# A gated recurrence and a long convolution on one core: the hand-kept order table searched anew, with no state copy on VectorE

## The chip, the cores and the metric

The kernel runs on one core of one Trainium2 chip. The core has five engines that run at the same time, each through a queue of its own in order: TensorE (PE in the profile, its weight loads apart as PEld), VectorE (DVE), ScalarE (ACT), GpSimd (POOL) and SyncE (SP), which here only issues DMA transfers. TensorE writes to PSUM, eight banks of 2 KB a partition; GpSimd works in SBUF alone. The metric is the device time of one execution in microseconds, lower being better, as the median of several runs.

## The reference

Four sequences of 6272 steps with 256 channels. A gated recurrence runs over time; its state is the input of three projections; the middle one is convolved over the whole sequence (circularly, through an FFT) with a filter per channel; the three are multiplied, and an output projection follows.

```python
sig = 1.0 / (1.0 + np.exp(-f_logit))
f = lower_bound + (1.0 - lower_bound) * sig
for t in range(S):
    h = f[:, t] * h + (1.0 - f[:, t]) * x[:, t]
    y[:, t] = h
proj = y @ w_proj                      # [.., 768]: x1, x2, x3
X2 = np.fft.rfft(x2, n=S, axis=1)
H = np.fft.rfft(filter_fft, n=S, axis=0)
x2_conv = np.fft.irfft(X2 * H, n=S, axis=1)
out = (x1 * x2_conv * x3) @ w_out
```

## The kernel before

The work is cut into 2430 small operations, each made of one or a few instructions, and created stage by stage in `prepare`, `hgrn`, `gate`, `spectrum` and `phase_o` through `plan.op`. An operation knows which engines can do it (`cost` has a planner's figure for each) and which operations it needs before it. The string `ORDER` is the whole plan: three characters an entry give an operation's number, its engine and its PSUM bank. `emit` walks through the table and issues each operation on the engine named there, so the table alone sets what stands behind what in every queue. "MUL" as an engine means VectorE with the next product folded in: the entry that GpSimd would have done then issues nothing.

The stages for each of the four batches:

- `hgrn`: 13 chunks of 512 steps. Two loads (`load`, L357) bring gate logits and x; ScalarE takes the sigmoid (L360), GpSimd multiplies (L362, "u"), TensorE turns both so that time runs along the free dimension (L374), ScalarE or VectorE forms the gate (L387, L389), and VectorE scans (L395, in two halves of the channels). The state of the first 3072 steps is needed once more behind the end of the sequence; the operation "wrap" copies it there, from SBUF to SBUF, 512 f16 values a partition (the helper `copy`: L289 on ScalarE, L294 on VectorE, L301 on GpSimd).
- `spectrum`: the projection of the middle third (L729, `phase_p`), which needs all scans and wraps of the batch and the zero fills of the buffer X2 (`pads`, L335 to L339); then the first step of the transform over the 128 blocks (L742), the second (L804), the product with the filter's spectrum, either on VectorE straight out of PSUM (L827) or as an evacuation with a product on GpSimd (L836), and back (L846). The spectra of the filter wait in DRAM and are loaded a unit at a time (L782).
- `gate`: the projections x1 and x3 (L423), their evacuations (L291, L294, L296, `XS`) and their product `zt`, on VectorE from PSUM (L444) or on GpSimd (L453).
- `phase_o`: the last inverse step (L909), in 13 groups of rows, the multiply with `zt` on VectorE (L915), the output projection (L927), its evacuation and the store (L939).

While batch b is in `spectrum`, `gate` and `phase_o`, the loads, multiplies and scans of batch b+1 run between them. Ahead of all that, `prepare` makes the tables (sines, masks), scales the weights W13 and W2 (operation "W", L291, L296, L303) and takes the filter's spectrum: 13 loads (L640), a copy of each in SBUF ("fr", L289, L294, L301), a rotation on TensorE (L651), an evacuation into `f2` ("f2"), whose gaps a copy fills ("pad" in the table, from `iden`), and two transform steps (L666, L684). Meanwhile TensorE runs matmuls that compute nothing (L618).

The helper that many of the operations share (its scaled form is L291, L296 and L303):

```python
def copy(e, dst, src, scale=None):
    if e == "ACT":
        nc.scalar.copy(dst, src)
    elif e == "DVE":
        nc.vector.tensor_copy(dst, src)
    else:
        nc.gpsimd.tensor_copy(dst, src)
```

Of the kernel before, what the change touches and what calls it, by code (L numbers as in the profile page):

```python
# [24 lines left out]
M = 128  # L25
# [37 lines left out]
class Plan:  # L63
# [63 lines left out]
    "AAYA4gBAgAiQAPYACIA0gADIAQIBIgA8gAdQBEgAkQBQgBMgAbQA5YAcQA6QA1IDogBYgBUgAeSBBYAgSBggAhSARAATYBCSAzAABIAfUBcgA2UApWA7"  # L127
    "IBDCAWYAXYA9IA+WAjQBkgAmQA3MBFIDrgDpgBJYBKQDsgBGSBLAAsUAoUEDgDqgAtUD3gAxUBNYA/OBRIBSUAlQArQAUIBHKAEgBTEASABOQAZSBVYA"
    "aCD4gBPAAnTAvTAYIBZIBaUBbMAqTAVYBhYAyTBWSBXCEbgBdIAuQBiQEEgBjIBeUAwSBlYBfEEPgDtABmSBnKBvUBqSBwEBoQEQgDuYBrKBxUBpIB6S"
    "EngEcgByMEFABtQB0UBsYBuAAFYBzYB7KDvWB1MD5AB4SB/QB5CDzUCAAB8YDwODxOD6YCBSEzgAGgD0ECKQCCCD1MB9WEdACESB+GCLICDYEGYD7UCF"  # L130
    "KCIQD8ECRWD/SCJAD9MERACPQCMYE9gEogEAKCSGESYCNUCQAEHWELQE0gFHgEBKCOECaSEMAFIgEeYEIOEJOCbCEpAE+gENICUUCYSETWCZCCVECdSE"
    "KYCTYEXQCeCAJYEUOEVOChUEYACiME1ACfSEfWEZICcYAIYEWYCoUCgCEgOE/ACqQCpMEqYCjYEjSCrAEhOCkUFbgFSgEkCFRgCxQCvWClECHgElKFJA"
    "CwGE2YAKYCsYCGgB3gErUCyICtSEsMEtMEvQCuCC6WEwAC0SEiYC7GE3UExIC1CC4WE4ME6QC5GFdAE5MC9WFAYFlgFcgCzYC8YAMYDISC+GE7IE8IDB"
    "UFmgC3gAHgDJCFBWC/SFCOFDOFKYFEQDCEFTAC2gALYDACCWgDKUFFACngFvgDESDLEFGIFLWDDYDFCDNUDMYFUYFwgB2gDHgDPQDOEFOSFMOFNODQAJ"
    "SUFnAFeYFVQFPKFQKDRWJUEFWAFYUDSGFXIDaSFZEFoYFfWDbCFaMJTQFgGFiSJVAFhODUUF5gCmgCXgMWgDGgFjCAOYFpQDVEANYDTYFkKDhWFxAFqA"
    "D2YEuYJXUDiOFsSJZEFrIDYWFtCEmYFyYMigDfUF+gDZGFuKFzQDgEDdWEOYF0AF2UMjgEyAECAGkgMXgMugF1IDkSEaYDyYDcYD+YF3MJYQDlCJcRF4"
    "MGQUGRMDeGJWYJaAF6YJbYF7YDmgGMSGUWJeJGNKDngG2gMvgMYAGVGGSUGCQGYSGDAGZCGTMGOWGKUDWgMkAGPOMlYDjYMZYGEQGIWGWSGLEGGUGJOG"
    "XKGFAMwAGHMGAWJdQJhRGBGJfAJiSG/gGtgDXgJjJJkqGcWGdGGgUJgYGhEGaQGbIJmSGeWMxYJnTGfGF8UJoKGlQJpLF9EJrSGuWGpoJqYGiUJtCGyG"
    "JsTGjMJwRJxXGnoJuDHIUGmYJyBGoYGzYGqYGvYHJEG3SGwuHSgHbgGrQG5CGsAJzvGxYHAUG4YJvYG7qG0WHOQG1GJ0YG6YHBYG8YHCsJ1TJ2SHPAHK"
    "WJ3LJ6UHLGHEsHMQJ7THNAG9WJ8MHkgHtgJ9rJ4CHTUHQQJ/SKATHDYJ5YHFYG+GHXEHRIHVsHGQKBCHcWHHAHWYKCrHlUHguHeuHnEJ+YKESKFTKGCH"  # L140
    "UYHdYKJUHYYHhYIAgKHDH2QHZSHfYKIYH3AKLMHiWIJgHaCHpsHqYHoYHmYHuQHyoKDYHwoHjGKKUH8SKMEH4WH6UHzYH9CHvYKNYHxYKORH7EHrSISg"
    "H5OIbgKQBIBUHsCH+WIFsMaQIDEIKSMbAIEYH/OMeUIOCMcIH0WM6gMfEKPTH1GMgMIkQICYIPYILYITWIlAIGYM7gIugKRrIcUIXGIMqIHQKSYIeEKT"
    "XIIAINYIYYIUYJlYIgMKVHIVuMmSMqQMnCIQUNGgMrAIWYMoKNHgIZWIREI3gJAgMsIIaGIvUM8AKUSIoWIzsIfYIhYI0YIdYIpGKYTImQKWqKZVInAI"
    "qWIxsKXYKdSMVgNTgKaDIyYM9YIiQNSgIrOKfCKeTIjAKgrKbtMyWIsQNIAI4SMzGItIKhYM2UNJYI6CKiQKjRM0OM3EKnSNegJJgM4MM+WORgNfgKkA"
    "I8CIwYKpCKoQKlpKqoKrYI7YKcYI9YKmYI5YM/GNCUNogNpgKsRNDENAOI1SKuBKtQKxRI2CNEMNUAJBWNKSKvoKzBI+UNVYJFuNLCNOQJDGNMKJGYI/"
# [867 lines left out]
```

## Time and profile before

| | |
|---|---|
| median of 3 runs | 461.9 us (461.58 to 461.95) |
| profiled execution, its own time | 461.1 us |
| its span, first to last instruction | 459.3 us |
| mean granted TensorE clock | 0.994 |
| DMA | 119.05 MB, mean 259 GB/s |

The profiled execution is one run among others, 0.8 us below the median; its span leaves out 1.8 us around the first and the last instruction. Busy time is counted per engine; a busy TensorE is not TensorE at its peak, since matmuls overlap. In the slices of the whole span (40 of them, in tenths) TensorE is below nine tenths in three:

```profile
PE   7999999999999999999999999999799999999994
DVE  6889997999999995999999979999899958999873
POOL 6569996977998952678997826999696804868400
```

The first slice is the preparation, the last the end of the last batch, and the slice between them with a 7 lies at 321 to 333 us.

### The profile page before, as it was taken

Reading aid. Unit: us, or ns where it says so; the run is one execution under the profiler, and the core shown is the slowest. Engines: PE = TensorE matmul, PEld = TensorE weight load, DVE = VectorE, ACT = ScalarE, POOL = GpSimd, SP = SyncE. Lnnn points to the kernel's source line nnn. Section 1 sums busy time; section 2 is a strip of 40 time slices with the busy share of each in tenths; the row PEclk is TensorE's granted clock in tenths of the full one; section 3 lists DMA queues with packets and bytes.
Section 4 is the critical chain, followed back from the end, with each engine's and each line's share of the span. In section 5 each row is a group of like instructions: output and inputs, shape, how many; then the busy total and the mean of one; then the engine's idle time right before and its main releaser. Section 6 shows DMA issues by size and latency. Waiting matters only on the chain.

```text
span 459.3 us, 14550 instructions
## 1 busy us (share of the span) xinstructions
PE 439.4 (96%) x6013; PEld 346.3 (75%) x6013; DVE 411.8 (90%) x458; ACT 389.0 (85%) x539; POOL 326.0 (71%) x308
## 2 busy tenths in 40 slices
PE   7999999999999999999999999999799999999994
PEld 5877778777667889867668898786568897766783
DVE  6889997999999995999999979999899958999873
ACT  4589999989999879999999878999589878997553
POOL 6569996977998952678997826999696804868400
PEclk9999999999999999999999999999899999999999
DMA  8998899658998655588998381899837532752167
GB/s 323 407 395 330 288 392 386 266 184 272 349 335 285 259 199 214 195 295 297 298 330 309 151 324 46 271 360 380 321 81 261 202 138 100 241 179 94 48 269 293
DMA packets 42563, 119.05 MB, mean 259 GB/s; under 512 B 4096, under 2 KB 5760, under 8 KB 42496
## 3 DMA queue, kind: packets, MB, share of 16 engines
q1 hardware_dynamic: 42496, 118.11, 70.3%
q8 instruction: 47, 0.77, 0.7%
q14 instruction: 20, 0.16, 0.1%
HBM read 86.12 MB, written 31.98 MB: 257 GB/s over the span
## 4 chain that ended last, share of the span: by engine, by line
PE 66%; DVE 19%; issue 6%; ACT 6%; POOL 2%; DMA 1%; DVEq 0%; ACTq 0%; POOLq 0%
PE PS L423 15%; PE PS L846 9%; PE PS L729 8%; DVE HA L395 8%; PE PS L374 7%; PE PS L804 6%; PE PS L927 6%; PE PS L742 6%; DVE ys L915 5%; DVE zt L444 3%; PE PS L909 3%; PE PS L666 2%; ACT X L289 1%; PE PS L618 1%; PE PS L651 1%
## 5 line engine op out<-in xcount | busy, mean ns | idle before, releaser
L395 DVE TENSOR_TENSOR_SCAN HA<-fTs,HA,PS 128x512 f16<-128x512 f32 (+1 forms) x96 | 112.8, 1201 | 2.4 <-ACT fTs L387 1.5
L423 PE MATMUL PS<-HA,W 128*128 128x490 f16 (+1 forms) x416 | 102.9, 367 | 0.6 <-DVE XS L296 0.2
L836 POOL TENSOR_TENSOR PP<-HA,Hu 98x1008 f16<-98x1008 f16 x46 | 96.3, 2104 | 8.7 <-issue 7.0
L289 ACT CAST HA<-PS 98x512 f16<-98x512 f32 (+1 forms) x107 | 84.7, 819 | 5.6 <-PE PS L804 1.5
L362 POOL TENSOR_TENSOR XT<-XT,FL 128x1024 f32<-128x1024 f32 (+1 forms) x31 | 67.1, 2166 | 25.4 <-ACT FL L360 16.4
L387 ACT ACTIVATE fTs<-PS,nomc 128x512 f32<-128x512 f32 (+1 forms) x87 | 57.2, 666 | 10.0 <-PE PS L374 6.1
L915 DVE TENSOR_TENSOR ys<-PS,zt 128x1024 fp32r<-128x1024 f32 (+1 forms) x52 | 58.4, 1151 | 6.5 <-PE PS L909 2.9
L827 DVE TENSOR_TENSOR PP<-PS,Hu 98x1008 f16<-98x1008 f32 x50 | 59.0, 1198 | 1.5 <-PE PS L804 0.5
L927 PE MATMUL PS<-Wo,ys 128*128 128x256 f32 x392 | 57.7, 293 | 2.4 <-DVE ys L915 2.1
L846 PEld LDWEIGHTS <-PP 98*128 98x128 f16 x1024 | 50.2, 98 | 10.9 <-issue 2.6
L362 POOL TENSOR_TENSOR X<-X 128x1024 f32<-128x1024 f32 x21 | 49.9, 2383 | 10.8 <-ACT X L360 10.7
L846 PE MATMUL PS<-FT,PP 98*128 98x98 f16 x1024 | 56.2, 207 | 0.5 <-POOL PP L809 0.2
L423 PEld LDWEIGHTS <-W 128*128 128x128 f16 x416 | 34.5, 97 | 27.9 <-issue 4.4
L289 ACT CAST Th<-PS 128x784 f16<-128x784 f32 x61 | 49.6, 819 | 6.9 <-PE PS L846 5.6
L927 PEld LDWEIGHTS PS<-Wo,ys 128*128 128x128 f32 x392 | 49.5, 188 | 7.7 <-DVE ys L915 3.1
L444 DVE TENSOR_TENSOR zt<-PS,XS 128x490 f16<-128x490 f32 (+1 forms) x81 | 51.1, 648 | 4.4 <-PE PS L423 1.6
L291 ACT ACTIVATE XS<-PS 128x490 f32<-128x490 f32 (+1 forms) x79 | 45.3, 583 | 4.1 <-PE PS L423 3.1
L453 POOL TENSOR_TENSOR zt<-XS 128x490 f16<-128x490 f32 (+1 forms) x23 | 25.9, 1128 | 29.7 <-DVE ys L915 23.5
L729 PE MATMUL PS<-W,HA 128*128 128x256 f16 x392 | 43.8, 273 | 0.0
L729 PEld LDWEIGHTS <-HA 128*128 128x128 f16 x392 | 42.9, 142 | 0.6
L742 PEld LDWEIGHTS <-X 128*128 128x128 f16 x512 | 31.5, 98 | 9.3 <-issue 2.8
L294 DVE CAST X<-PS 128x1024 f16<-128x1024 f32 (+1 forms) x21 | 25.2, 1224 | 14.7 <-PE PS L729 13.3
(111 smaller groups left out, 801.4 us busy)
## 6 DMA issues: line engine op xcount, KB each, us to landing
Hu<-H SPq DMA_DIRECT2D x39, 512.0 KB, 5.4
FL<-in_f_logit_dram SPq DMA_DIRECT2D x27, 512.0 KB, 5.7
XT<-in_x_dram SPq DMA_DIRECT2D x27, 512.0 KB, 7.1
out_dram<-osb SPq DMA_DIRECT2D x24, 512.0 KB, 5.2
X<-in_f_logit_dram SPq DMA_DIRECT2D x21, 512.0 KB, 6.8
X<-in_x_dram SPq DMA_DIRECT2D x21, 512.0 KB, 6.9
out_dram<-PP SPq DMA_DIRECT2D x16, 512.0 KB, 5.2
Hl<-H SPq DMA_DIRECT2D x13, 512.0 KB, 4.3
```

What stands on the lines that cost most here:

```text
L289: nc.scalar.copy(dst, src)
L362: op("u", {"POOL": 0.1 + 0.553 * nb}, lambda e, xt=xt, ft=ft: nc.gpsimd.tensor_tensor(xt, xt, ft, op=AOP.mult), r=[("ft", k)], w=[("xt", k)])
L395: nc.vector.tensor_tensor_scan(h, fT, bank(pb)[:, 512 - hn:512 + hn], init, op0=AOP.mult, op1=AOP.add),
L423: nc.tensor.matmul(PS[:, p, 0:n], W13[:, kh, js], HA[:, HB[kh] + t0:HB[kh] + t0 + n], start=(kh == 0), stop=(kh == 1))
L444: nc.vector.tensor_tensor(zd(), px, xs(0), op=AOP.mult)
L729: nc.tensor.matmul(pp[:, r - r0, :], column(HB[kh], q_of(r)), W2[:, kh, :], start=(kh == 0), stop=(kh == 1))
L742: nc.tensor.matmul(pa[:, i, :], X2[:, j:j + 128], D1, start=True, stop=True)
L827: nc.vector.tensor_tensor(pr, px.unsqueeze(1).broadcast_to([TB, 2, UE, 63]), hh(), op=AOP.mult)
L836: nc.gpsimd.tensor_tensor(pr, spec[:, o, :, 1:64].unsqueeze(1).broadcast_to([TB, 2, UE, 63]), hh(), op=AOP.mult)
L846: nc.tensor.matmul(PS[:, ib + o, pr * TB:(pr + 1) * TB], PP[:TB, k, o, n, 2 * pr:2 * pr + 2, :], v[:TB], start=(n == 0), stop=(n == 1))
L915: nc.vector.tensor_tensor(late["ys"][:, yk, :, 0:rn * 128], PS[:, cb:cb + 2, 0:rn * 128], late["zt"][:].rearrange("p k r m -> p k (r m)") ...
L927: nc.tensor.matmul(po[:, i, :], late["ys"][:, yk, kh, i * 128:(i + 1) * 128], Wo[:, kh, :], start=(kh == 0), stop=(kh == 1))
```

## The change

The string `ORDER` is another one; nothing else in the file differs. The search that made the new table held every copy of VectorE from SBUF to SBUF while GpSimd works, and allowed no wrap on VectorE. The operations, their instructions and the buffers are the same; what differs is the engine of 156 of the 2430 operations, the order in the queues (of a TensorE operation by one place in the mean, at most 14), and the PSUM banks.

```diff
@@ -124,69 +124,69 @@
 ORDER = (
-    "AAYA4gBAgAiQAPYACIA0gADIAQIBIgA8gAdQBEgAkQBQgBMgAbQA5YAcQA6QA1IDogBYgBUgAeSBBYAgSBggAhSARAATYBCSAzAABIAfUBcgA2UApWA7"
...
+    "AAYAPYA4gA0gA5YABIACIADIAQIBAgBIgA8gA1ABMgBEgDogAiQAdQAkQAbQAcQAeQAgQA6QAhSAfSA2SARAATIA7IAWYAXABBYBCUBDEASAApWBJIAj"
...
 )
```

Read as operations, the changes of engine that are not paired off by a change back within the same kind are:

```text
wrap   batch 0: 2 from ACT to POOL     batch 3: 1 from DVE to POOL
W      DVE +1 (128x512, half of W13), POOL -1
pad    the filling of f2's gaps, ACT to DVE
masks  POOL to DVE (six instructions of one column)
fr     ACT +2, DVE -1, POOL -1
f2     ACT +2, DVE -2
A, Th  ACT +3, DVE -3
f      ACT +3, DVE -3
o      DVE +1, ACT -1
prod   ACT -2, DVE +1, MUL +1
xs     ACT -3, DVE -1, MUL +4
x2     batch 0: ACT +2, DVE -2; batches 2 and 3: DVE +1 and ACT -1 each
rest, idw, tabs   one each between ACT, DVE and POOL
```

On GpSimd the wrap of batch 3 that VectorE did stands behind the last multiply of that batch, ahead of the zero fills. In the last `phase_o`, TensorE's operations of row groups 9 to 11 stand so, before and after ("I1" is L909, "proj" L927, the number the row group):

```text
before  I1 9, proj 10, proj 9, I1 11, I1 12, proj 11, proj 12
after   I1 9, proj 10, I1 11, proj 9, proj 11, I1 12, proj 12
```

More of the change, by code (lines that the diff above doesn't have):

```diff
@@ L131 @@
[L131 to L145, printed above, removed]
@@ new lines @@
+    "WAmWAsWBKWA9YA+QAoUBFYA3KAVIAtUBQgBYgDpgBUgBggAZUBLGAzIA/IAxVAlVBGWBRABSQArVBcgBkgDrgDqgDsgEDgD3gAEgD4gEbgEEgEPgEcgA"
+    "nVBHGAaMBNIAvVAYYBOUBTABZIBaQAqWAyWAUYBhYBVIBWWAuSBiSBPEBXGBjCBdIBbIBeWBlYBmSAwQBfGDtABnKBqWBxSByKBoQBrOBpABvUBwMEFA"
+    "DuYBsYBzYAFYB6SBtWBuGB0UD5AB7KB1MDvQB4SDwIDxIB5CCBWDzUCCGEzgEQgD0EB/SCACD1MB8YD6YCKWEGYCDYB9QCLOCESD7UCFKEdAB+AD8ECI"
+    "WCJGD/QCPSERACQCCRWCSGD9MCNUEHSCOEEAIEBICUWCYQELUEIKEJKCVGCaWEeYCMYCTYCZAE1ACbGESYE0gEngCcYE2YCfQChSAHgE9gEogE+gFHgE"
+    "MMENMCiKCgAETWCdQEXUEpAEUOEVOAOYCjYEqYCeACoSEYECkQEZMCpCEfWClACvSEgOE/ACqUCrEEjQEkACwKEhOCxSErUCyKElICtWFJAEvSEsEEtM"
@@ new lines @@
+    "CuGC4QEwCExKE3WC6UAGgFIgFRgCsYFAYCzYC5AE4GC7EEiYEKYAIYC0QE5OE6SC1AC/UE7KDBWFTADAMDCGE8KFBQC9UFCAFEWC+EFKYFDIDKSC8YEW"
+    "YAJYAKYDDYFFGDIUDLCDJEDEQDFAALIFGOFSgB3gAMYEuYCXgFcgFUYB2gFbgCGgFlgFvgFmgC3gCWgFwgC2gFLSFOUFMKFNKFPEDPWDQGFdAFQMANYD"
+    "MYFeYDaQDNWFVSFYUFWKFXKDOGDbAFZEFnAFaMDRWJSQFfSJUADSGFxAJTRJXQJVBFiWFgKFjGDUUDVEJZIFhKFkOEOYFoYD2YDTYFyYFpQDhSFsUDfW"
+    "FqAFrIDiCDYSFtEDgGDZCFuMFzQDkWF0AF2SDdUCmgGkgMWgMXgCHgMigDXgMugDGgDlGDeEF5gDngMvgMYADWgCngDmgF+gMjgDHgF1IG2gGtgG/gEa"
+    "YDyYD+YEmYDcYDjYEyYECYJWYMZYF6YF7YJYQJcRF3KF4KGWSGSUGXCJeBJaoGUWGGSGQQGRIGVGGHCGTEGEWGISGMQGYUMwAGJCMkAGNAGFOGZMGKWG"
@@ new lines @@
+    "LOGASGCUGDEGBKMlYMxYGOQGPAJdWJhXJiSGcQGdAJfuGgUJjPJkqGaWGbGGhMGeSGfCJmQJnRJoIJppF8WGlUF9GGpsGuSGiQGyCG3WGjIG5GJrTJsV"
+    "GnsJtDHIQGwqJwTJxWJuFJyDJzuGmYGqYGvYGoYJ0YGzYGrUGxYG7uHJAHASG0QHEqGsEG1AJ1WHOUJ2XHPEHKQJvYG4YG8YG6YHFYHBYJ3OHCqHDYJ6"
+    "THLAHMUHSgHbgJ7WHkgHtgHNEG9QJ8LJ4vHTSG+AHQUJ/XJ9uHRMHGQHXCKBHHVqHcUHHAHlWKAQKERHgsHnGH2SKFVKCoHesKGBHUYHfYHhYHYYHWYH"
+    "dYHZQHpuKHFH3CKIYHqYHoYHmYKJWHiUHuSHaAKLOHjEKKXKMHH4QHyqHwqH5AKNYHvYH6UH8WH9GKOTKQDH7MHrQIBWHsAIAgH+UIDuMaSIFGIJgH/M"
+    "IKQMeWHzYIGYHxYMbCIOAMcKMfGH0UKPRH1EMgOIkSKRpIMoINYILYIEYITUICYISgIbgIHWIXsM7gM6gIugIlCIVEIIGKTRKVBMmSMnCIcWIgOMoKMq"
@@ new lines @@
+    "QIeGIPYJ+YIUYIWYIYYMrAIQUIZWIREKUSMsIKYTImUIvQKWqKaLIxoIzoIaGM8AIyYIfYJqYIhYKDYIdYIoWInEIqSKZUKdVKfNKbsIpGIiWIrCIjGN"
+    "GgMyQMVgJAgNHgI3gNogNSgNTgIsSItKMzAKeVM2WKiUKjSKnTNfgF/gNegJJgI0YMhYORgM9YIwYI5YNIAKcYNJYM0IM3GKgtKkEI4QM4OKpDM+UI6A"
+    "KoTM/EKlqNCWKqrI8AKsSNDGNAMNEOKuCJBQJFANUAKtTI1UKxRKySJDoKzBK0qKvrJEYI7YI2EK1YNKWNOQKwYI9YJgYNVYJ5YI+UJCYJGYKmYNLGJl"
+    "YNPANMOI/EK2TK3SJKWK7UK8VNQIK4DNgAJMGK9EK5qNWQNaSJOuLAUK+tNXANbCLCENYINcKJHWJIGLBVLFULDtLHEJbYNhYK6YKhYJLYJPYJNYNiQL"
+    "GWLKULIuNlSNjANqANkILLVLMEObgOQgNpgU5gNygNzgLNtJQWN8gN9gNmCJRGLPULQQR1RR2VLUWNnKLRER3BR4FLSoKXYK/YKSYM5YLOYNrYKrYNsS"
```

89 lines of the change are left out of this document (42 added, 47 removed).

## The prediction

> **What bounds the kernel now.** I read the page first, then the groups with their shapes kept apart, the chain of waits in order of time, and short stretches where TensorE idles.
>
> ```profile
> PE 439.4 (96%) x6013; PEld 346.3 (75%) x6013; DVE 411.8 (90%) x458; ACT 389.0 (85%) x539; POOL 326.0 (71%) x308
> PE 66%; DVE 19%; issue 6%; ACT 6%; POOL 2%; DMA 1%; DVEq 0%; ACTq 0%; POOLq 0%
> ```
>
> TensorE and VectorE share the bound: the chain changes between them, and neither rests for long. So a reordering has no large idle stretch to fill, and what counts are single holes. The groups show the odd one (columns: count, busy us, mean ns, idle before):
>
> ```profile
> L294 DVE COPY HA<-HA 128x512 f16<-128x512 f16 x1 | 3.9, 3885 | 0.0
> L301 POOL COPY HA<-HA 128x512 f16<-128x512 f16 x45 | 26.4, 615 | 0.0
> ```
>
> This is the one wrap that VectorE does: 3.89 us, where GpSimd copies the same shape in 0.62. Around it, from the timeline (start, us, engine) and from stretches of 2 us (busy PE, PEld, DVE, ACT, POOL, then the granted clock, DMA share, GB/s):
>
> ```profile
> 317.97 2.36 POOL L362 TENSOR_TENSOR XT<-XT,FL 128x1024 f32<-128x1024 f32 x1
> 319.10 3.88 DVE L294 COPY HA<-HA 128x512 f16<-128x512 f16 x1
> 320.49 2.35 POOL L362 TENSOR_TENSOR XT<-XT,FL 128x1024 f32<-128x1024 f32 x1
> 322.79 2.15 POOL L836 TENSOR_TENSOR PP<-HA,Hu 98x1008 f16<-98x1008 f16 x1
> ```
>
> ```profile
> 320.00:322.00 2.00, 0.79 (x16) 0.50 (x12) 2.00 (x1) 1.42 (x3) 2.00 (x3) 1.00 1.04 383
> 322.00:324.00 2.00, 0.00 (x0) 0.00 (x0) 1.90 (x3) 0.00 (x0) 2.00 (x2) 1.00 1.04 424
> 324.00:326.00 2.00, 1.61 (x24) 1.50 (x25) 1.77 (x3) 0.46 (x1) 1.02 (x2) 0.58 1.01 408
> 326.00:328.00 2.00, 2.00 (x30) 1.66 (x29) 1.37 (x2) 1.10 (x3) 0.25 (x1) 0.57 1.03 397
> ```
>
> The copy ends at 322.98, just as the GpSimd instruction that began at 320.49 ends (322.84). It was waiting, not working. Behind it TensorE and ScalarE run dry, and when TensorE comes back it is granted 0.58 of its clock for some 4 us. The chain of waits passes through it:
>
> ```profile
> 319.18 3.80 DVE HA L294
> ...
> 324.39 1.12 PE PS L374 x16
> ```
>
> **The change part by part.** Only the table differs: engines, places in the queues, PSUM banks.
>
> *The wrap leaves VectorE.* On the chain that is 3.80 us. The scalings, the gate multiply and TensorE's transposes behind it (L296, L444, L374) come sooner by that. Bounds: TensorE's idle time at that place, 3.60 us in the next fence, and 3.88.
>
> *The slow clock after the hole goes too.* Equal groups at the low and at the full clock:
>
> ```profile
> 324.39 0.69 PE L374 MATMUL PS<-idc,FL 64*128 64x64 f32 x8 [3.60 <-DVE zt L444]
> 325.44 1.49 PE L846 MATMUL PS<-FT,PP 98*128 98x98 f16 x16
> 326.86 1.02 PE L804 MATMUL PS<-HA,FT 64*128 64x256 f16 x8
> 328.21 0.60 PE L804 MATMUL PS<-HA,FT 64*128 64x256 f16 x8
> 328.64 0.41 PE L374 MATMUL PS<-idc,FL 64*128 64x64 f32 x8
> 330.89 0.88 PE L846 MATMUL PS<-FT,PP 98*128 98x98 f16 x16
> ```
>
> (0.69 - 0.41) + (1.49 - 0.88) + (1.02 - 0.60) = 1.31 us, on TensorE's part of the chain. Bounds: 0 if VectorE (idle little here) sets the pace, 1.3. I take it whole, since the chain lies on PE there. Together -5.1. Three stretches of equal kind, from the start of one batch's projection (L729) to the next, agree:
>
> ```profile
> 72.60:167.90 95.30, 93.53 (x1376) 72.81 (x1374) 89.43 (x95) 88.23 (x126) 81.14 (x69) 1.00 0.75 273
> 167.90:266.00 98.10, 96.63 (x1421) 76.33 (x1419) 91.29 (x98) 89.22 (x126) 71.87 (x63) 1.00 0.73 262
> 266.00:369.10 103.10, 98.48 (x1441) 78.88 (x1439) 97.48 (x102) 89.95 (x127) 76.97 (x62) 0.98 0.70 254
> ```
>
> Per matmul they take 69.3, 69.0 and 71.5 ns; with 5.1 us off, the third takes 68.0.
>
> *The same wrap on GpSimd* (0.62 us) now stands behind that batch's last multiply, ahead of the zero fills. The fills end before the projection that waits for them begins (369.10 above):
>
> ```profile
> 365.09 0.14 POOL L339 MEMSET X<- 128x16 f16 x1
> ```
>
> 3.9 us of cover hide it: 0, and 0.6 if the cover were gone. Two ScalarE wraps of batch 0 that go to GpSimd have the same answer.
>
> *The end.* In the last batch the table puts the inverse transform of row group 11 (L909) ahead of group 9's output projection (L927) on TensorE; today it stands behind:
>
> ```profile
> 449.67 1.18 PE L927 MATMUL PS<-Wo,ys 128*128 128x256 f32 x8 [0.33 <-DVE ys L915]
> 450.78 0.74 PE L909 MATMUL PS<-ID,Th 64*128 64x128 f16 x20
> 451.50 1.56 DVE L915 TENSOR_TENSOR ys<-PS,zt 128x1024 fp32r<-128x1024 f32 x2 [0.85 <-PE PS L909]
> ```
>
> The multiply at 451.50 could start some 1.4 us sooner (L927's 1.18 plus its wait of 0.33, less what remains of the earlier multiply). Bounds -1.4 and 0, since ScalarE must have freed the bank first. I take the middle, -0.7.
>
> *The prologue.* The filling of f2's gaps (1920 elements a partition) goes from ScalarE to VectorE, with the six mask instructions, while two copies of filters (`fr`) go to ScalarE.
>
> ```profile
> 6.06 1.95 ACT L289 CAST f<-iden 128x1920 fp32r<-128x1920 f16 x2
> ...
> 10.56 0.69 DVE L294 CAST afs<-X 128x1024 fp32r<-128x1024 f32 x1
> ...
> 12.30 1.60 DVE L294 CAST afs<-X 128x1024 fp32r<-128x1024 f32 x1
> 12.32 1.04 POOL L301 CAST afs<-X 128x1024 fp32r<-128x1024 f32 x1
> 24.82 2.71 PE L666 MATMUL PS<-D1r,f 128*128 128x256 f32 x20 [0.87 <-DVE f L294]
> ```
>
> A copy of 1024 takes 0.69 us alone and 1.60 beside a GpSimd instruction, so 0.9 of holding. The filling is then about 1.3 us alone, 2.2 held, and lies ahead of evacuations that L666 waits for at 24.82; two `f2` evacuations and a filter copy fewer on VectorE make room for it. Bounds -0.5 (that room is worth something) and +2.2; I take +0.5, nearer the row of the copy that ran alone.
>
> *Half of W13 on VectorE.* One scaling of 128x512 inside SBUF, in batch 0's scans, goes from GpSimd (1.62 us) to VectorE. It stands between the two scans at 57.02, so it comes up at 58.24 (half of their 2.45 later), with eleven scans of that batch queued behind it, and the projection behind those:
>
> ```profile
> 56.41 1.62 POOL L303 TENSOR_SCALAR W<-HA,omc 128x512 f16<-128x512 f32 x1
> 57.02 2.45 DVE L395 TENSOR_TENSOR_SCAN HA<-fTs,HA,PS 128x512 f16<-128x512 f32 x2
> 58.59 0.21 POOL L675 CAST mX<-afs 128x16 fp32r<-128x16 f32 x1 [0.41 <-ACT afs L289]
> 58.77 4.72 POOL L362 TENSOR_TENSOR X<-X 128x1024 f32<-128x1024 f32 x2
> 63.45 2.37 POOL L362 TENSOR_TENSOR XT<-XT,FL 128x1024 f32<-128x1024 f32 x1
> ```
>
> On the chain of waits those two scans stand as well:
>
> ```profile
> 57.02 1.34 DVE HA L395 x2
> ```
>
> Alone: half of 0.69, so 0.35 us. GpSimd has a pause of 0.41 us there, in which it fits. Held as in the prologue: 0.35 + 0.9 = 1.25. I take 0.8; the upper end is the slower rival below.
>
> *All else* (some 150 copies, evacuations and products changing engine, mostly in pairs, and shifts of a few places). From group means VectorE gets about 0.4 us less besides the wrap (two casts of 1.22 fewer, three gates, four z products of 0.66 more), ScalarE 2 us more of 389, GpSimd some 10 us less. The 69.3, 69.0 and 68.0 ns say how far different orders of this work differ: up to 1 ns or 1.4 us a batch to either side, about 2 us over four. I take 0.
>
> Sum for the profiled execution (span 459.3, its own time 461.1): -5.1 - 0.7 + 0.5 + 0.8 = -4.5, so 456.6. The median of the runs, 461.9, lies 0.8 above that execution, so I forecast 457.4.
>
> **The rivals.**
>
> *The hold comes back at W13 (slower).* If VectorE reaches that scaling after GpSimd's pause, which ends at 58.59, it can be held through 58.77 to 65.82, three multiplies without a pause: 7.1 us, with the scans on the chain there. For it: the wrap was held past one GpSimd boundary (the multiply from 317.97 ended at 320.33) until 322.98. Against it: GpSimd's own queue has lost that 1.62 us, and a scaling has not been seen held. Time: 457.4 - 0.45 + 7.1 = 464.1. It turns the result slower once the hold passes 4.9 us. [...]
>
> *Transfers give the gain back.* The DMA share is 1.01 to 1.04 in the four stretches above, so loads would not come sooner though the work does. Against it:
>
> ```profile
> 320.06 0.38 SPq L782 DMA_DIRECT2D Hl<-H  x1
> ...
> 338.50 2.11 POOL L836 TENSOR_TENSOR PP<-HA,Hl 98x1008 f16<-98x1008 f16 x1
> ```
>
> The last spectrum load issued there is used 18 us later. If half of 5.1 were lost: 460.0.
>
> *No gain.* The hole at 320 is filled by another of like size, because 1.4 us a batch is lost in the new order in each of three batches: -4.5 + 4.2, so 461.6. The 68 to 69 ns speak against three losses at once. [...]
>
> **How the numbers follow.** Forecast 0.62, hold at W13 0.20, transfers 0.08, no gain 0.10. The likeliest case by itself, with the bounds added as squares (end 0.7, prologue 1.0 down and 1.7 up, W13 0.45, order 2): 455.0 to 460.1. The range goes to 454.4 below and 463.0 above, which takes in the second and third rival and the shorter holds. About 0.2% or 0.9 us is what a measurement can tell from no change: faster 0.68 (nearly all of the first case, most of the transfers'), same 0.10, slower 0.22.
>
> **What would show it.** Right: no VectorE copy of 128x512 f16 in the groups; no TensorE gap above 1.5 us and no clock under 0.9 between two projections in the last batch; that stretch at 97 to 99 us; the multiply of row group 11 with less idle time before it; the W scaling under 1.3 us. Wrong: a W scaling or a copy on VectorE of several us near 58, L666 starting after 26, or all three stretches longer per matmul.

## The result and the profile after

The changed kernel takes 454.5 us (median of 6 runs, 453.42 to 456.81) against 461.7 (median of 6, 461.30 to 461.95): 7.2 us less at the medians. The ratio of the runs is 0.9853, 95% interval 0.9829 to 0.9877, by which the gain is 6.8 us. The forecast was 457.4 with a range of 454.4 to 463.0. Its direction and its likeliest cause were right; the time came out 2.9 us below the forecast, below the 455.0 to 460.1 of the likeliest case by itself and only 0.1 us inside the range. That it lies inside at all is in part luck.

The page of the profiled execution (its own time 454.32 us, span 452.1), first the busy times, then the chain that ended last:

```profile
PE 435.6 (96%) x6013; PEld 345.1 (76%) x6013; DVE 404.9 (90%) x463; ACT 393.1 (87%) x542; POOL 315.1 (70%) x296
PE 68%; DVE 14%; ACT 7%; DMA 5%; issue 4%; SPq 1%; ACTq 0%; DVEq 0%
```

VectorE's share of the chain falls from 19% to 14%, and DMA's rises from 1% to 5%: something new is waited for. On the page 3 of the 5 are a store (`out_dram<-HA`) and 2 a load of the filter in the preparation. The stretches of 2 us in which TensorE ran dry before (busy PE, PEld, DVE, ACT, POOL, granted clock, DMA share, GB/s):

```profile
320.00:322.00 2.00, 1.91 (x48) 1.78 (x45) 1.97 (x3) 2.00 (x4) 2.00 (x1) 1.00 1.03 408
322.00:324.00 2.00, 2.00 (x37) 1.24 (x33) 1.89 (x2) 2.00 (x5) 2.00 (x2) 1.00 1.07 421
324.00:326.00 2.00, 2.00 (x24) 1.26 (x23) 2.00 (x3) 1.99 (x4) 2.00 (x3) 1.00 1.01 393
```

TensorE is busy all through, at full clock; from batch 2's first projection to batch 3's its longest wait is 0.6 us, where it was 3.6. The same view from projection to projection:

```profile
70.76:165.05 94.29, 93.18 (x1376) 72.86 (x1374) 87.91 (x96) 87.21 (x123) 74.89 (x64) 1.00 0.78 273
165.05:264.86 99.81, 97.13 (x1419) 76.50 (x1417) 90.72 (x97) 91.73 (x130) 72.46 (x59) 1.00 0.73 261
264.86:363.13 98.27, 97.39 (x1444) 77.64 (x1442) 93.97 (x102) 88.35 (x124) 78.35 (x67) 1.00 0.71 254
```

From the first start of L729 in each batch, and the same for the experiments' profiles (us; "end" is the rest of the span):

| kernel | first projection | stretch 1 | stretch 2 | stretch 3 | end | span |
|---|---|---|---|---|---|---|
| before | 72.6 | 95.3 | 98.0 | 103.2 | 90.2 | 459.3 |
| changed | 70.8 | 94.3 | 99.8 | 98.3 | 89.0 | 452.1 |
| e1, wrap on GpSimd | 72.3 | 95.5 | 98.0 | 98.3 | 89.6 | 453.7 |
| e4, start of the new table | 72.5 | 96.2 | 98.0 | 104.5 | 89.7 | 461.0 |
| e5, two filter copies | 71.4 | 95.1 | 98.0 | 103.3 | 89.4 | 457.2 |
| e11, filling besides | 72.0 | 95.1 | 98.0 | 104.9 | 89.5 | 459.4 |
| e14, e1 and e5 together | 71.3 | 96.2 | 98.0 | 98.5 | 89.3 | 453.2 |
| e6, changed, store sooner | 70.7 | 94.3 | 98.1 | 98.3 | 88.9 | 450.3 |

The gain of 7.2 us in span is -1.8 before the first projection, -1.0, +1.8, -4.9, and -1.2 at the end. The shorter preparation and both changes in stretches 1 and 2 had not been forecast. In the preparation (VectorE, then TensorE):

```profile
11.63 2.11 DVE L294 CAST f<-iden 128x1920 fp32r<-128x1920 f16 x2
...
15.45 0.68 DVE L294 CAST afs<-X 128x1024 fp32r<-128x1024 f32 x1
16.05 0.68 DVE L294 CAST afs<-Hu 128x1024 fp32r<-128x1024 f32 x1
17.57 0.69 DVE L294 CAST afs<-Hu 128x1024 fp32r<-128x1024 f32 x1 [0.83 <-PE PS L651]
...
22.91 2.42 PE L666 MATMUL PS<-D1r,f 128*128 128x256 f32 x17 [0.34 <-DVE f L294]
```

The filling takes 2.11 us, as long as was feared, and yet L666 starts at 22.91, 1.9 sooner than before. The filter copies behind it take 0.68; before, the groups of the like copies had means of 1.20, 1.07 and 0.88. In batch 1, ScalarE and TensorE wait for a store, which stands on SyncE's queue behind two loads:

```profile
166.94 1.20 SPq L357 DMA_DIRECT2D XT<-in_x_dram  x2
168.18 1.38 SPq L939 DMA_DIRECT2D out_dram<-HA  x1
...
179.80 1.93 ACT L289 CAST HA<-PS 128x1024 f16<-128x1024 f32 x2 [2.74 <-DMA out_dram<-HA]
...
180.86 0.61 PE L804 MATMUL PS<-HA,FT 64*128 64x256 f16 x8 [1.19 <-ACT HA L289]
```

The scaling of W13 that moved to VectorE, with the GpSimd scaling beside it:

```profile
55.10 0.61 DVE L296 TENSOR_SCALAR W<-HA,omc 128x512 f16<-128x512 f32 x1
...
55.07 0.84 POOL L303 TENSOR_SCALAR W<-HA,omc 128x128 f16<-128x128 f32 x1
```

It wasn't held for a whole GpSimd instruction. No run has this scaling alone; one of 128x520 in f32 takes 0.43 in the preparation, and the GpSimd scaling beside it took 0.84 where the others of its shape take 0.61 to 0.64, so each may have waited some 0.2 us for the other. And the end (VectorE's last multiplies):

```profile
441.76 1.23 DVE L915 TENSOR_TENSOR ys<-PS,zt 128x1024 fp32r<-128x1024 f32 x1 [0.34 <-PE PS L909]
444.59 1.23 DVE L915 TENSOR_TENSOR ys<-PS,zt 128x1024 fp32r<-128x1024 f32 x1 [1.61 <-PE PS L927]
447.40 0.42 DVE L915 TENSOR_TENSOR ys<-PS,zt 128x256 fp32r<-128x256 f32 x1 [1.58 <-PE PS L909]
```

Group 11's inverse step is early, but its multiply at 444.59 still waits for L927, group 9's projection: both use the same `ys` buffer. Group 12's inverse step has come to stand behind group 11's projection, and VectorE waits 1.58 us for it.

### The profile page after: what moved, and what is told of

Read it like the earlier page. It is cut to its first block, busy times and chain, and to the rows that moved or that the text cites. A ratio compares the mean times of both kernels' runs of the same rounds, so it can differ in the third digit from the quotient of the medians.

```text
span 452.1 us, 14540 instructions
## 1 busy us (share of the span) xinstructions
PE 435.6 (96%) x6013; PEld 345.1 (76%) x6013; DVE 404.9 (90%) x463; ACT 393.1 (87%) x542; POOL 315.1 (70%) x296
## 3 DMA queue, kind: packets, MB, share of 16 engines
q1 hardware_dynamic: 42496, 118.11, 72.5%
## 4 chain that ended last, share of the span: by engine, by line
PE 68%; DVE 14%; ACT 7%; DMA 5%; issue 4%; SPq 1%; ACTq 0%; DVEq 0%
PE PS L423 18%; PE PS L846 10%; PE PS L374 8%; PE PS L729 7%; DVE HA L395 7%; PE PS L804 6%; PE PS L927 6%; PE PS L742 5%; DVE ys L915 4%; PE PS L666 3%; ACT HA L289 3%; DMA out_dram<-HA 3%; PE PS L909 3%; DMA Hu<-in_moe_filter_fft_dram 2%; PE PS L684 1%
## 5 line engine op out<-in xcount | busy, mean ns | idle before, releaser
L836 POOL TENSOR_TENSOR PP<-HA,Hu 98x1008 f16<-98x1008 f16 x45 | 94.3, 2104 | 5.4 <-ACT HA L289 2.6
L289 ACT CAST HA<-PS 128x1024 f16<-128x1024 f32 (+1 forms) x107 | 85.2, 829 | 6.8 <-DMA out_dram<-HA 2.7
L387 ACT ACTIVATE fTs<-PS,nomc 128x512 f32<-128x512 f32 (+1 forms) x90 | 59.5, 672 | 6.6 <-DVE HA L395 2.4
L827 DVE TENSOR_TENSOR PP<-PS,Hu 98x1008 f16<-98x1008 f32 x51 | 60.2, 1198 | 1.5 <-issue 0.5
L927 PE MATMUL PS<-Wo,ys 128*128 128x256 f32 x392 | 57.8, 293 | 2.6 <-DVE ys L915 2.4
L444 DVE TENSOR_TENSOR zt<-PS,XS 128x490 f16<-128x490 f32 (+1 forms) x85 | 54.0, 650 | 4.4 <-PE PS L423 2.7
L927 PEld LDWEIGHTS PS<-Wo,ys 128*128 128x128 f32 x392 | 49.4, 188 | 7.5 <-ACT PP L291 1.6
L289 ACT CAST Th<-PS 128x784 f16<-128x784 f32 x62 | 50.7, 820 | 4.2 <-PE PS L846 3.0
L729 PE MATMUL PS<-W,HA 128*128 128x256 f16 x392 | 43.8, 273 | 0.1
L729 PEld LDWEIGHTS <-HA 128*128 128x128 f16 x392 | 42.9, 142 | 0.5
L289 ACT CAST X<-PS 128x1024 f16<-128x1024 f32 (+1 forms) x31 | 30.7, 1040 | 10.9 <-PE PS L729 10.7
L453 POOL TENSOR_TENSOR zt<-XS 128x490 f16<-128x490 f32 (+1 forms) x19 | 21.8, 1148 | 24.8 <-DVE ys L915 18.8
```

The source lines that it names most:

```text
L387: nc.scalar.activation(fT, sT, AF.Identity, scale=by, bias=1.0)
L729: nc.tensor.matmul(pp[:, r - r0, :], column(HB[kh], q_of(r)), W2[:, kh, :], start=(kh == 0), stop=(kh == 1))
L827: nc.vector.tensor_tensor(pr, px.unsqueeze(1).broadcast_to([TB, 2, UE, 63]), hh(), op=AOP.mult)
L836: nc.gpsimd.tensor_tensor(pr, spec[:, o, :, 1:64].unsqueeze(1).broadcast_to([TB, 2, UE, 63]), hh(), op=AOP.mult)
L927: nc.tensor.matmul(po[:, i, :], late["ys"][:, yk, kh, i * 128:(i + 1) * 128], Wo[:, kh, :], start=(kh == 0), stop=(kh == 1))
```

## The experiments

Each is an edit of the table, told as operations (number, kind, engine). Their tables fill two lines fewer, so their line numbers are 2 lower: L292 is L294 of the kernels above. Each was compared with runs of the kernel before on its own chip (medians 461.6 to 461.8).

### The wrap: four places for one copy

**e1**, the old table, the wrap on GpSimd:

```diff
-1919 wrap DVE   behind 1756 xs
+1919 wrap POOL  ahead of 1927 wrap
```

> The table of before with one entry altered: the wrap that VectorE did goes to GpSimd, behind the last multiply of its batch. Theory (the held copy costs its 3.8 us on the chain and 1.3 us of slow clock): 461.7 - 5.1 = 456.6 us, no TensorE idle stretch of 3.6 us in the last batch and no clock below 0.9 there, the stretch between the last two projections 98 us instead of 103. Rival (the gain of the change is the reordering's, the hole would be filled by the next wait): 460 us or more.

Measured: 455.92 (4 runs), ratio 0.9874 [0.9858, 0.9890], so -5.85 us; the third stretch falls to 98.3. This one copy carries most of the change. It is 0.75 more than the 5.1 worked out, and the runs of before suggest why: of the 15 beside this kernel, the nine whose mean granted clock was 0.988 or 0.989 have a median of 462.2, the six at 0.992 to 0.995 one of 461.2, and the forecast worked with the trace of an execution at 0.994. E4 below, with the same hold of 3.88 us and the same wait of 3.60 us on TensorE behind it, has a trace at 0.989; there the low clock after the hole lasts longer:

```profile
322.00:324.00 2.00, 0.00 (x0) 0.00 (x0) 2.00 (x2) 0.33 (x1) 2.00 (x2) 1.00 1.03 417
324.00:326.00 2.00, 0.76 (x14) 0.76 (x16) 1.90 (x3) 0.00 (x0) 1.79 (x1) 0.68 1.05 422
326.00:328.00 2.00, 2.00 (x28) 1.67 (x26) 1.51 (x3) 0.87 (x2) 0.34 (x1) 0.50 1.00 394
328.00:330.00 2.00, 2.00 (x30) 1.70 (x28) 1.61 (x2) 1.57 (x3) 0.47 (x1) 0.50 1.04 396
330.00:332.00 2.00, 2.00 (x25) 1.41 (x20) 1.28 (x1) 1.83 (x4) 1.93 (x2) 0.61 0.83 326
```

I read the figures between 0.50 and 1.00 as means over a change: in stretches of 0.2 us of the trace of before the clock is 0.50 or 1.00 but for the two in which it changes (0.79 and 0.68). By that it is 0.50 for 3.4 us in before (324.3 to 327.7), and, worked out from the means of stretches of 2 us, for 6.8 us in e4 (324.7 to 331.6) and e8 (323.9 to 330.8; means of 0.98, three times 0.50, and 0.81 from 322 to 332). The mean clocks of these three profiles are 0.994, 0.989 and 0.989; e5's is 0.993 and e11's 0.989, which fits 3.4 us at the low clock in e5 and 6.8 in e11, an estimate from the means alone. Stretch 3 takes 103.2 us in before and 103.3 in e5, 104.5 to 104.9 in e4, e8 and e11.

**e2**, the old table, the wrap still on VectorE, but where GpSimd waits for ScalarE:

```diff
-1919 wrap DVE   behind 1756 xs
+1919 wrap DVE   ahead of 1829 y
```

> The table of before with the same wrap left on VectorE, but moved 30 places down its queue, to where GpSimd waited for ScalarE for 2.2 us (348.3 to 350.5 in the trace of before). Theory (the copy was waiting for GpSimd, not working): the copy takes 0.2 to 0.4 us there and the time is that of the wrap on GpSimd, 456.6 to 457.0 us. Rival (a 512-element copy inside SBUF is slow on VectorE by itself): 3.5 us or more for the copy wherever it stands, and 459 us or more.

Measured: 456.32, ratio 0.9882 [0.9868, 0.9895], the copy 0.27 us:

```profile
344.59 0.27 DVE L292 COPY HA<-HA 128x512 f16<-128x512 f16 x1
```

GpSimd's multiply there starts only at 345.74, after 2.25 us of waiting. So the engine VectorE was not the trouble by itself; the copy was short where GpSimd paused. The copy itself took 0.27 here, and 3.6 of its 3.88 us were waiting.

**e8**, the old table, the wrap one place earlier (a single run):

```diff
-1919 wrap DVE   behind 1756 xs
+1919 wrap DVE   ahead of 1756 xs
```

> The kernel before with VectorE's wrap one place sooner in VectorE's queue, ahead of the product it followed, so that it comes up some 0.6 us earlier within the same GpSimd multiply (317.97 to 320.33). Theory: whether VectorE gets in at a boundary between GpSimd's instructions depends on the moment; the copy may then take about 1.9 us (in at 320.33) or 4.5 us (in at 322.84, as before). Rival, by which a hold lasts one whole GpSimd instruction: 1.9 us at most. One look at the copy's length; the time follows it, 459 to 460 with 1.9 and 461.5 to 462.5 with 4.5.

```profile
318.38 4.45 DVE L292 COPY HA<-HA 128x512 f16<-128x512 f16 x1
...
317.83 2.35 POOL L360 TENSOR_TENSOR XT<-XT,FL 128x1024 f32<-128x1024 f32 x1
320.14 0.33 POOL L807 TENSOR_TENSOR PP<-zp 98x32 f16<-98x32 f16 x1
320.34 2.33 POOL L360 TENSOR_TENSOR XT<-XT,FL 128x1024 f32<-128x1024 f32 x1
324.91 2.10 POOL L834 TENSOR_TENSOR PP<-HA,Hu 98x1008 f16<-98x1008 f16 x1 [2.24 <-ACT HA L287]
```

It comes up 0.7 us sooner and ends with the same GpSimd instruction as before: the multiply from 320.34 runs to 322.67, the copy to 322.83. Two boundaries, at 320.2 and 320.5, pass it by again. Here GpSimd has nothing to do at 322.67 (it waits for ScalarE), so this trace doesn't show the copy let in between two instructions; that of before does, at 322.8. The rival, one whole GpSimd instruction, falls. The time of the single run was 462.36.

**e3 and e13**, the new table, the wrap on VectorE again, at two places:

```diff
-1919 wrap POOL
+1919 wrap DVE   behind 1756 xs     (e3)
+1919 wrap DVE   behind 1655 prod   (e13)
```

> The new table with that one wrap put back on VectorE, behind the same gate multiply as before. Theory (the copy is held as long as GpSimd runs without a pause, whatever the order around it): the copy takes 2 to 6 us and the time rises by as much and up to 1.5 us of slow clock, 457 to 461 us. Rival (the hold was an accident of the old order): under 1 us for the copy, 454.5 to 455 us.

> The new table with the wrap on VectorE as in the run on it (454.1, the copy 0.30 us long), but two places later, so that it comes up near 320.2, inside a GpSimd multiply (318.93 to 321.30) with two spectrum products of 2.1 us behind it. Theory: the moment of arrival decides; inside the multiply it is held for 1.4 us if the first boundary lets it in, for 3.1 us or more if it is passed over as in the kernel before, and the time is 455.2 to 457.5. Rival: the new table has the cover that the old one lacked (the hole is filled by other engines' work): the copy is long, but the time stays within 0.5 us of 454.1.

Measured: e3 454.09, ratio 0.9831 [0.9818, 0.9845]; e13 455.08, ratio 0.9851 [0.9829, 0.9873]. Neither copy was held. From e3's timeline:

```profile
317.62 0.30 DVE L292 COPY HA<-HA 128x512 f16<-128x512 f16 x1
...
315.40 2.37 POOL L360 TENSOR_TENSOR XT<-XT,FL 128x1024 f32<-128x1024 f32 x1
317.72 0.40 POOL L807 TENSOR_TENSOR PP<-zp 98x32 f16<-98x32 f16 x1
```

I had expected a hold, as the wrap stands behind the same operation as in the old table. It arrived at the end of a multiply and got in at that boundary, where the next GpSimd instruction took 0.40 in place of 0.33. In e13, four places further down VectorE's queue, it was to arrive inside a multiply:

```profile
318.59 1.20 DVE L825 TENSOR_TENSOR PP<-PS,Hu 98x1008 f16<-98x1008 f32 x1
319.70 0.28 DVE L292 COPY HA<-HA 128x512 f16<-128x512 f16 x1
...
318.65 3.55 POOL L360 TENSOR_TENSOR XT<-XT,FL 128x1024 f32<-128x1024 f32 x1 [0.65 <-ACT FL L358]
```

The expectation failed in the other direction: the copy took 0.28, and GpSimd's multiply 3.55, where the 48 multiplies of this shape in the kernel before have a mean of 2.38. That extra 1.17 us runs from the multiply's start at 318.65 to about the copy. VectorE's product ahead of the copy had begun 0.06 us before the multiply and took 1.20. I read it so: GpSimd was kept out for the copy before the copy began. That the product by itself kept it out is the rival; against it, in the trace of before the same kind of product from 317.41 lies over the start of the multiply at 317.97, which took 2.36. This rests on one trace and was not tried further. The time is 1.0 us above e3's, with intervals that overlap.

So "a copy of VectorE beside GpSimd costs 3.9 us" isn't a price. It was 0.27 to 0.30 in three places and 3.88 to 4.45 in two, and in one of the three GpSimd's multiply was the longer one.

### The preparation

**e4**, the first part of the new table up to the first projection, then the old one:

```diff
-402 entries of the old table
+402 entries of the new table
 the rest as in the old table, without those
```

> The new table up to the first projection of batch 0 (the preparation and the first scans), and the table of before for all that is left. Theory (the new start is worth what the traces show, the first projection at 70.8 instead of 72.6 us, and the rest follows it unchanged): 461.7 - 1.8 = 459.9 us. Rival (the later stages take the gain back, since they wait for loads whose times do not move): 461 us or more.

Measured: 461.13 (11 runs), ratio 0.9991 [0.9977, 1.0006]: no gain, against my expectation. The table is not in order of time, so the seam may shift work on other queues. The start of L664 came out at 23.9, the first projection at 72.5, a filter copy on VectorE was held beside GpSimd, and the filling and GpSimd's filter copy lengthened each other:

```profile
10.00 1.20 DVE L292 CAST afs<-X 128x1024 fp32r<-128x1024 f32 x1 [0.79 <-PE PS L649]
...
12.66 2.08 DVE L292 CAST f<-iden 128x1920 fp32r<-128x1920 f16 x2
...
12.74 1.97 POOL L299 CAST afs<-X 128x1024 fp32r<-128x1024 f32 x1 [2.09 <-PE PS L649]
```

This splice moved too much at once to tell why the start is quicker; e5 moves less.

**e5**, the old table, two filter copies from GpSimd to ScalarE, so that VectorE's copies beside them run free:

```diff
-73 fr POOL
-77 fr POOL
+73 fr ACT
+77 fr ACT
```

> The kernel before with two filter copies (fr) of the preparation on ScalarE in place of GpSimd, nothing else. Theory: the first of the changed kernel's gains (first projection at 70.8 in place of 72.6) comes from VectorE's own filter copies, which GpSimd's copies beside them held (1.60 and 1.46 us for 0.69 alone); here those two take 0.69 each, the transform step that waits for them starts some 1.5 us before 24.8, the first projection at about 71.1, and the time is 460.2. Rival: the loads set the pace of the preparation, a hold there is waited out anyway: the step starts at 24.8 and the time is 461.7. If ScalarE is the late one then (each copy costs it about 1 us), it is 462 or more.

Measured: 459.53, ratio 0.9947 [0.9932, 0.9963]; the first projection at 71.4, as expected:

```profile
12.21 0.69 DVE L292 CAST afs<-X 128x1024 fp32r<-128x1024 f32 x1
13.94 0.68 DVE L292 CAST afs<-Hu 128x1024 fp32r<-128x1024 f32 x1
23.64 2.71 PE L664 MATMUL PS<-D1r,f 128*128 128x256 f32 x20 [0.88 <-DVE f L292]
```

The two copies took 1.60 and 1.46 before. The second of them in the trace of before, beside a GpSimd copy from 14.83 to 15.87:

```profile
14.96 1.46 DVE L294 CAST afs<-Hu 128x1024 fp32r<-128x1024 f32 x1
```

1.7 us of holding gone brings the transform step 1.2 us forward. The median gains 2.2, of which the trace shows 1.2 here; most of the rest of the span's 2.1 lies in the end, 89.4 for 90.2. The other profiles with the old end have 89.3 to 90.0 there, so the execution of before was long at that place. Why the medians differ by 1 us more than this part of the trace is open. The rival, that the loads set the pace there, falls.

**e11**, e5 with the filling on VectorE:

```diff
 73 fr ACT
 77 fr ACT
-51 pad ACT
+51 pad DVE   behind 63 f2
```

> The kernel before with the two filter copies on ScalarE, as in the run on them (459.5), and the filling of f2's gaps on VectorE besides, behind its third evacuation. It prices the forecast's step for the filling by itself: the forecast took +0.5 us (bounds -0.5 and +2.2). Theory: the filling takes 1.3 us alone or 2.2 held, and the first transform step waits for VectorE's evacuations behind it, so it starts 1.3 to 2 us later than the 23.64 of that run, and the time is 460.8 to 461.5. Rival: VectorE waits 2.26 us for TensorE ahead of 19.18 in that run, a pause in which the filling vanishes, and ScalarE is eased by 1.95 us: 459.0 to 459.5.

Measured: 461.00, ratio 0.9985 [0.9970, 1.0000], 1.5 above e5 as the theory had it, but the trace puts only part of that at the filling:

```profile
13.79 1.23 DVE L292 CAST f<-iden 128x1920 fp32r<-128x1920 f16 x2
24.02 2.71 PE L664 MATMUL PS<-D1r,f 128*128 128x256 f32 x20 [0.87 <-DVE f L292]
```

L664 comes 0.4 us later and the first projection 0.55; stretch 3, which still has the wrap's hole in it, is 1.6 longer, at a mean clock of 0.989 over the execution, where e5's has 0.993. Most of e11's runs have the lower clock (0.989 or 0.990), most of e5's the higher (0.992 or 0.993), which was worth 1.0 us among the runs of before. So the filling, unheld, costs about half a microsecond where it stands, and the rest goes with the lower mean clock. Whether the filling has a part in that was not tried.

### The scaling of W13

**e12**, the changed kernel, the scaling five places later on VectorE:

```diff
-11 W DVE   behind 323 scan
+11 W DVE   behind 342 f
```

> The changed kernel with VectorE's scaling of half of W13 later in its queue, behind the gate of that batch's fourth chunk from the end, so that it comes up near 60.7, inside a GpSimd multiply (59.62 to 61.99), with a copy and a further multiply of GpSimd right behind (61.92 and 62.59 to 64.96); this is the forecast's slower rival, made to happen. Theory: as with the wrap, VectorE isn't let in at the first boundary: the scaling takes 1.9 us (in at 62.5) or 4.2 us (in at 64.96), the scans behind it are late by as much less the 0.35 it works, and the time goes from 454.5 to 455.5 to 458. By one whole GpSimd instruction it takes 1.3 to 1.6 us and the time is 455.2. Rival: a scaling with its operand from f32 isn't held at all: 0.6 us and 454.5.

Measured: 456.61 (455.10 to 457.80), ratio 0.9883 [0.9855, 0.9911]:

```profile
60.33 1.64 DVE L294 TENSOR_SCALAR W<-HA,omc 128x512 f16<-128x512 f32 x1
...
59.31 2.37 POOL L360 TENSOR_TENSOR X<-X 128x1024 f32<-128x1024 f32 x1 [0.31 <-ACT X L358]
61.62 0.82 POOL L299 COPY HA<-HA 128x512 f16<-128x512 f16 x1
```

So a scaling is held as well, from 60.33 to the end of the multiply at 61.68, and goes in there; the GpSimd copy behind it, 0.61 elsewhere, takes 0.82. This is the one-instruction case, seen in one trace. The first projection follows 1.1 us later (71.9), the hold of 1.0 us passed on in full, and the spans differ by that (453.2 and 452.1); the medians are 2.1 apart. Of e12's four runs, the two with a mean clock of 0.997 and 0.998 took 455.1 and 455.5, the two at 0.993 took 457.7 and 457.8; no trace was taken of the latter, so what they lose is not shown.

### The late store and the last groups

**e6**, the changed kernel, one store of batch 0 ahead of the two loads on SyncE:

```diff
 1350 load SP, 1338 load SP
-753 store SP   behind them
+753 store SP   ahead of them
```

> The changed kernel with one store of batch 0's output put on SyncE's queue ahead of the two loads it stands behind. Theory: the 1.8 us that the changed kernel loses between the first and second projection-to-projection stretch comes from ScalarE's wait of 2.74 us for this store near 179.8 (the buffer the store reads is written next), on which TensorE then waits 1.19 us; without it the stretch of batch 1 takes 98.0 to 98.6 us in place of 99.8 and the time is about 453.0. Rival: the wait is covered by other work, as ScalarE is not the bound: within 0.3 us of the changed kernel's 454.5. A second rival: the two loads now come later and hold up the next batch by as much: 454.5 or above.

Measured: 453.47 (452.65 to 454.07), ratio 0.9819 [0.9801, 0.9836]. The store goes first, and ScalarE waits for TensorE only:

```profile
166.86 0.48 SPq L937 DMA_DIRECT2D out_dram<-HA  x1
167.38 1.63 SPq L355 DMA_DIRECT2D XT<-in_x_dram  x2
...
177.99 1.93 ACT L287 CAST HA<-PS 128x1024 f16<-128x1024 f32 x2 [1.00 <-PE PS L740]
```

Stretch 2 is back at 98.1. The median gains 1.0 us, not 1.5, and the intervals of this ratio and of the changed kernel's overlap, so the gain is not clear. The other profiles of the new table fit that. The store stands in the same late place in e3, e7, e12 and e13; ScalarE's wait for it was 0, 1.9, 2.1 and 0 us there, and stretch 2 took 98.1, 99.2, 99.8 and 98.0. It is a wait that some executions have. The place on the queue alone doesn't make it: the store was issued at 168.2 in the changed kernel, and later, at 168.9 and 169.3, in e3 and e13, where nobody waited; what differs is when it landed: 11.5 us after its issue in the changed kernel, within 9.3 and 8.9 us in e3 and e13, where ScalarE's copy began at 178.2. So e6's trace without the wait doesn't yet show that the edit removed it. The wait may be part of why the changed kernel's runs spread over 3.4 us; those of e6 spread over 1.4.

**e7**, the changed kernel, the inverse step of group 12 ahead of group 11's projection:

```diff
-2425 I1 PE   behind 2422 proj
+2425 I1 PE   behind 2412 proj, bank 4 (2427 proj in bank 2, in exchange)
```

> The changed kernel with the inverse step of the last row group (12) on TensorE ahead of the output projections of groups 11 and 9's successor, in a bank of its own. Theory: the forecast's step at the end got only part of its gain because the multiply of group 11 shares a buffer with group 9 and because group 12's inverse step came to stand behind group 11's projection (VectorE idle 1.58 us there); with it ahead, the multiply of group 12 follows that of group 11 at once (at 445.9 in place of 447.4) and the end comes 0.4 to 0.8 us sooner: 453.9. Rival: the store of group 11, which stays where it is, ends last, and nothing is won: 454.5.

Measured: 454.52 (4 runs), ratio 0.9842 [0.9826, 0.9858]: nothing won. Both last multiplies now run together, and VectorE's last evacuation stands beside ScalarE's:

```profile
445.21 1.55 DVE L913 TENSOR_TENSOR ys<-PS,zt 128x1024 fp32r<-128x1024 f32 x2 [1.60 <-PE PS L925]
448.10 0.42 DVE L294 TENSOR_SCALAR osb<-PS 128x256 f32<-128x256 f32 x1 [1.33 <-PE PS L925]
447.86 1.02 ACT L289 ACTIVATE osb<-PS 128x1024 f32<-128x1024 f32 x1 [1.68 <-PE PS L925]
```

From group 11's multiply to the end of the span it is 7.5 us in both kernels (445.21 to 452.7; 444.59 to 452.1). Group 12's wait of 1.58 us was covered by what follows group 11. That its store of 512 KB is what ends last fits this, but was not tried by itself.

### The two holds together

**e14**, the old table with the edits of e1 and e5, three engines in all:

```diff
-1919 wrap DVE, 73 fr POOL, 77 fr POOL
+1919 wrap POOL  ahead of 1927 wrap
+73 fr ACT, 77 fr ACT
```

> The kernel before with three engines changed and nothing else: the wrap on GpSimd (alone: 455.9, -5.9) and two filter copies on ScalarE (alone: 459.5, -2.2). Theory: the two holds are independent and the changed kernel's gain of 7.2 us is made of them, while the other 150 moves of the new table come to nothing in sum (a gain in the first batch, a loss by the late store in the second): 453.7, with the first projection at 71.4 and all stretches from batch to batch at 95 to 98.5. Rival: the gains overlap or the other moves carry a part of them, so that the time stays above the changed kernel's 454.5: 455 or more.

Measured: 454.65 (454.24 to 454.94), ratio 0.9848 [0.9835, 0.9862]; the changed kernel has 0.9853 [0.9829, 0.9877]. The sum would have been 453.7, and 1 us of the gains is lost in stretch 1 (96.2 for 95.1 in e5), for a reason that no run here shows. But three engines changed in the old table do as much as the whole new table.

## Why the forecast was right, and where it was too small

- **The wrap's hold and the slow clock, -5.1.** Right: stretch 3 lost 4.95 in the two profiles, and the wrap alone gives -5.85 in medians. Mis-sized in one point: the bound of 1.3 for the clock came from one execution with 3.4 us at the low clock, and others have 6.8. Of the 52 runs of before beside the experiments, 30 have a mean clock of 0.988 or 0.989, as the traces with 6.8 us have. With that goes the step that added 0.8 to come from the profiled execution to the median: without the hole, the changed kernel's profiled execution lies only 0.1 below its median. That much of the 0.8 belonged to the hole fits this and is not shown by itself.
- **The wrap on GpSimd at nothing.** Right: e1 needs no more than the changed kernel in stretch 3.
- **The preparation, +0.5.** This step failed. The filling was priced rightly (0.55 later at the first projection in e11, where it wasn't held). What the step left out were the holds that a reordering can take away. The row of 1.60 us for a filter copy stood in the prediction, but as a price for the filling, not as 0.9 us to win back. Two such copies set free were worth 1.2 us in e5's trace and 2.2 in its median. How the new table comes to 1.9 at L666 is not taken apart: it frees these copies, but lengthens another VectorE instruction ahead of them (L563, 1.41 us for 0.70), and e4 with the same start had L664 only 0.9 sooner. Together with W13's +0.8, the forecast had the first projection 1.3 later; it came 1.8 sooner.
- **Half of W13 on VectorE, +0.8, and the slower rival.** The scaling took 0.61, so 0.2 less than taken. The rival's mechanism exists (e12), but its price was 1.0 us of hold, not 7.1: it was let in at the first boundary. The wrap, which the forecast counted as held past one boundary, had passed two, since a short GpSimd instruction (320.28 to 320.62) lies between the multiplies. E12's hold ended within one multiply; that of the wrap in e8 didn't, 4.45 us past two boundaries. Neither the traces nor the forecast tell which it will be.
- **The end, -0.7.** The part after the last projection shortened by 1.2 against the execution of before, which was long there; against e1, with the old end, by 0.6. The size was near, the step's account not: "could start some 1.4 us sooner" overlooked that groups 9 and 11 share a `ys` buffer. Its own sign, less idle time before group 11's multiply, did not come: 1.61 us for 0.85.
- **All else, 0 with 2 us either way.** In the profile it was -1.0 in stretch 1 and +1.8 in stretch 2, where ScalarE waited for a store that had been moved behind two loads. "Shifts of a few places" didn't look at SyncE's queue. The second is a wait that only some executions have, and is gone in e6's trace; the first stands in every profile with the new table's first batch (94.3) and is left open.
- **Transfers, no gain.** Neither rival came: no load held up stretch 3. Of the DMA wait that appeared on the chain, 3% of the span are a store's and 2% a filter load's in the preparation.

From the forecast of 456.6 for the profiled execution to its 454.32: preparation and W13 -3.1, stretch 1 -1.0, stretch 2 +1.8, hold +0.15, end -0.5, and 0.4 more outside the span (2.2 in place of 1.8).

## What to carry to other kernels

When a profile shows one instruction far above the mean of its shape, look for every smaller case of the same kind: here the copies of 1.2 to 1.6 us in the preparation were worth 1.2 to 2.2 us beside the big one's 5.9, and three changed engines gave what a search over the whole table gave. A term for what a row costs must be asked both ways, as a price of what is added and as a gain of what goes. And when operations are reordered, compare the DMA queue too: a store moved behind two loads became a wait of 2.74 us on ScalarE here, since its buffer was written next.

## What the runs showed of the hardware

How long a copy inside SBUF on VectorE was held beside GpSimd did not follow from the two instructions alone: the same wrap, with GpSimd multiplies of the same shape beside it, took 0.28 to 0.30 us (e3, e13) or 3.88 to 4.45 (before, e8). Held to the first boundary: the scaling of e12, 1.64 for 0.61. Held past two boundaries between back-to-back instructions: the wrap, 3.88 and 4.45. Not held, with GpSimd lengthened instead: 0.28 for the copy and 3.55 for a multiply of 2.4. What decides between the first two is open: the instruction (a scaling from f32, a copy of f16), the moment of arrival and GpSimd's neighbours all differ. In e4's preparation both were long at once: the filling 2.08 for 1.23, and GpSimd's filter copy beside it 1.97 for 1.04.

The granted clock after a hole also varies between executions, and in these traces in two sizes: 0.50 for 3.4 us (before) or for 6.8 us (e4, e8), behind waits of TensorE of 3.60 us (3.25 in e8). In before TensorE was at work again from 324.39, within 0.1 us of the fall at 324.3. By the stretches of 2 us it came back at 325.2 in e4, 0.5 us after the fall at 324.7, and at 323.4 in e8, ahead of the fall at 323.9, but waited another 0.65 us at the low clock there. So the low clock was short where TensorE worked from the fall on, and long where it still waited behind it, in these three traces. The fall came 3.5, 3.1 and 3.7 us after TensorE had run dry (before, e4, e8). What sets the two lengths is not shown.
